# One weighting of the values for all heads in the even steps of a two-layer recurrent attention loop

## The chip, the cores and the metric

The kernel runs on one core of one Trainium2 chip. A core has TensorE (PE in the profile, its weight loads PEld), VectorE (DVE), ScalarE (ACT), GpSimd (POOL) and SyncE (SP), which here issues nearly all DMAs. TensorE writes its results to PSUM, which has eight banks of 512 fp32 numbers on each of 128 partitions; VectorE and ScalarE copy them to SBUF. The metric is the device time of one execution in microseconds (us).

## The reference, cut to what matters

Two layers, each of a recurrent attention with memory (A) and a dense block with relu (B), with the same weights in both, over 2048 tokens of 512 numbers.

```python
def _A_ref(x, mem0, Wq, Wk, Wv, Wo, seg_len):        # 32 heads of 128, M = 8 rows of memory, seg_len = 32
    mem = mem0
    for s in range(n_seg):                           # 64 segments
        xs = x[:, s * seg_len:(s + 1) * seg_len, :]
        h = jnp.concatenate([mem, xs], axis=1)       # L = 40 rows
        q, k, v = (jnp.einsum('btd,dhe->bhte', h, W) for W in (Wq, Wk, Wv))
        scores = jnp.where(mask, jnp.einsum('bhqe,bhke->bhqk', q, k) * scale, -1e9)
        o = jnp.einsum('bhqk,bhke->bhqe', softmax(scores), v)
        o = jnp.einsum('bhte,hed->btd', o, Wo)
        mem = o[:, :M, :]                            # handed to the next segment
        outs.append(o[:, M:, :])
    return jnp.concatenate(outs, axis=1)

x = x + _A_ref(_layernorm(x), ...)
x = x + _B_ref(_layernorm(x), B_w1, B_w2)            # relu(x w1) w2, inner width 1376
x = x + _A_ref(_layernorm(x), ...)
x = x + _B_ref(_layernorm(x), B_w1, B_w2)
```

A segment needs the memory that the one before it left, so the 64 segments of a layer follow each other.

## The kernel before, in words

The loop has 68 steps (`step(k)`, L801). In step k layer 0 works on segment k and layer 1 on segment k - 4 (`DELTA`), side by side: a = 0 and a = 1 are two columns blocks of 40 in the products of Q and K, two halves (rows 0 to 39 and 64 to 103) of the transposed probabilities and of the values `Vs`. The 32 heads are taken in two halves of 16, hf = 0 and hf = 1. In one step TensorE does, in this order:

- Q and K of the 16 heads of half 0 (`qp`, L663), in three batches, each copied out by ScalarE (Q) and VectorE (K);
- the values of the memory rows for all heads (`vp` from `rT`, L332), and in even steps those of layer 1's own segment (`values1`); they go by DMA through DRAM into the rows of `Vs`;
- the scores of half 0 (`sp`, L703); their exponents and probabilities follow on VectorE, ScalarE and GpSimd (L718 to L738);
- Q and K of half 1;
- the transposition of half 0's probabilities (`transpose_p`, L747), copied into `PT` in two parts, one by VectorE, one by ScalarE (L748);
- the scores of half 1;
- the weighting of the values of half 0 (`weighted_v`, `pv`, L762): for each head and layer one product of 40 rows and 40 columns, 32 matmuls in four banks;
- work of other kinds that fills the time until half 1's probabilities are there: the next values of layer 1 (`v1`), and where `fills_v0(k)` holds those of layer 0 three segments ahead (`v0`), products of the dense block (`dense_h`, `hp`; `dense_y`, `yp`), output projections (`output_x`, `wox`);
- the transposition of half 1, again into `PT`, a piece of filling work behind it, and the weighting of half 1;
- the projection of the memory rows of all heads (`output_mem`, `sp` from `OTm`, L710, written into the bank of layer 0's scores), whose result, copied by ScalarE and transposed (`mt`, L1097), becomes the memory of the next step (`HT`, L1100), with filling work in between.

The order on TensorE, VectorE, ScalarE and SP is that of the program text. Where the filling work lies is written out by hand: `places(i)` (L426) tells which heads of an output projection stand in which of four gaps of a step, and `hs` (L1010) does so for the 11 chunks of the dense block. The gaps are: after the values; between the second transposition and the weighting; after the memory projection; after `mt`.

Even steps are of two kinds. With k % 4 == 2 the step computes v0 and a whole dense_h and has no output projection; with k % 4 == 0 it has the rest of an output projection and neither v0 nor dense_h.

The weighted values of a head are split in the copies out of PSUM: the first `ahead(k, a)` columns (8, and 24 for layer 1 where k % 4 is 0 or 1 in most of the loop) go to `OTm` (`outputs_m`, L785), the others to `OTx0` (half 0) or `OTx1` (half 1) (`outputs_x`, L793). Half 0 is copied by ScalarE in both parts, half 1 by ScalarE for `OTm` and VectorE for `OTx1`.

PSUM: three banks `ps_c` (Q and K, transpositions, most weightings), two `ps_fill`, one `ps_wo` for the output projection, two for the scores (`sp_banks`). `VmS` of v0's second group is copied out by a function that is called later, behind the second transposition (L1027).

Of the kernel before, what the change touches and what calls it, by code (L numbers as in the profile page):

```python
# [22 lines left out]
def kernel(  # L23
# [327 lines left out]
    def values0(s, ii):  # L351

        if ii == 0:
            vds[0, s] = dram_values("vd0", "vd0", 4)
        t = tokens_T(s, 0, SEG)
        return group_values(lambda c4: t[:, c4, :], ii, vds[0, s], *((ps_fill, "fill") if ii else (ps_c, "c")), nc.sync,
                            "xn" if ii == 1 and s > 5 else "VmS", later=ii == 1 and s > 5)

    def values1(k, ii, place="VmS"):

# [58 lines left out]
    def fills_v0(k):  # L419

        return k % 2 == 0 and k + 3 < NSEG and k + 3 not in set_of

    def places(i):  # L426

        if i % 2 == 0:
            return (0, 10, 16, 24, H), (H,) * 5
        if i == NT - 1:  # L430
            return (0, 12, 12, 12, 12), (12, H, H, H, H)
        if fills_v0(2 * i + 2):
            return (0, 6, 10, 14, 20), (20, 23, 26, 30, H)
        return (0, 6, 10, 13, 16), (16, 23, 26, 30, H)

    def output_order(i):
# [301 lines left out]
        eng.tensor_tensor(out=P[:, :, 64 * a:64 * a + L], in0=es[:],  # L738
                          in1=sm[:].unsqueeze(2).to_broadcast([128, 8, L]), op=ALU.mult)

    def transpose_p():

        for p, copy in ((0, nc.vector.tensor_copy), (1, nc.scalar.copy)):
            tp = ps_c.tile([128, 4, 2, L], F32, tag="c")
            for sl in range(4):
                c = PL * (4 * p + sl)
                nc.tensor.matmul(tp[:, sl], lhsT=Pf[:, c:c + 128], rhs=ident_q, start=True, stop=True)  # L747
            copy(out=PT[:, 4 * p:4 * p + 4], in_=tp[:])  # L748

    def weighted_v(hf, act):  # L750
        pvs = {}
        for q in range(2):
            h0 = 16 * hf + 8 * q
            for a in act:
                pool, tag = (ps_fill, "fill") if (hf, q, a) in ((0, 0, 0), (1, 1, 1)) else (ps_c, "c")
                pvs[q, a] = pool.tile([128, 8, L], F32, tag=tag, name="pv")
            for hh in range(8):
                sl, g2 = divmod(8 * q + hh, 2)
                h = h0 + hh
                for a in act:  # L760
                    R = 64 * a
                    nc.tensor.matmul(pvs[q, a][:, hh, :], lhsT=Vs[R:R + L, h * Dh:(h + 1) * Dh],  # L762
                                     rhs=PT[R:R + L, sl, g2, :], start=True, stop=True)
        return pvs

# [35 lines left out]
    def step(k):  # L801
# [176 lines left out]
        with tc.high_priority(offset=PRIO):  # L978
            transpose_p()
            scores(qks[:2], act)  # L980
            scores(qks[2:], act)
            pvs = weighted_v(0, act)

            outputs_x(k, 0, pvs, 0, nc.scalar.copy)
            outputs_m(k, 0, pvs, 0)
            ess = exponents(act)


# [10 lines left out]
        if not apart:  # L999
            v1(1)  # L1000
        with tc.high_priority(offset=PRIO):
            outputs_m(k, 0, pvs, 1)
            outputs_x(k, 0, pvs, 1, nc.scalar.copy)
        v0(0)
        evict_v0 = v0(1)
        if k == 2:
            set_values(4, 3, 5)
            set_products(4, 5)
            set_store(4, nc.sync, 2, 4)
        hs = (0, 0, 4, 8, NFC) if fills_v0(k) else (0, 6, 8, 8, NFC) if len(act) == 1 else (0, 8, NFC, NFC, NFC)  # L1010
        if sooner is not None:
            dense_h(sooner, *hs[0:2])
        final = k == NSTEP - 1
# [6 lines left out]
        with tc.high_priority(offset=PRIO):  # L1020
            for a in act:
                probabilities(1, ess, a, k)
            if first:
                hand_on(dw)
            transpose_p()
            if evict_v0 is not None:
                evict_v0()  # L1027
            if k == 0:
                set_evict(3, 4)
                set_products(3, 5)  # L1030
            if k == 1:
# [12 lines left out]
        if nw is not None:  # L1044
            output_x(nw, *nx[1:3])
        with tc.high_priority(offset=PRIO):
            pvs = weighted_v(1, act)
            for q2 in range(2):
                if cont:
                    outputs_m(k, 1, pvs, q2)  # L1050
            head = act[:1] if nx is not None and nw % 2 == 0 else act
            outputs_x(k, 1, pvs, 0, nc.scalar.copy if final else nc.vector.tensor_copy, head)
            if first:
                block_normalize(dw)
            outputs_x(k, 1, pvs, 1, nc.vector.tensor_copy, head)
            for q2 in range(2):
                outputs_x(k, 1, pvs, q2, nc.vector.tensor_copy, [a for a in act if a not in head])
# [145 lines left out]
```

## Time and profile before

| | |
|---|---|
| runs (3) | 1613.30, 1613.77, 1613.97 us, median 1613.77 |
| profiled execution | 1612.95 us, of which the span from the first to the last instruction is 1611.2 |
| mean granted clock of TensorE | 1.000 |
| busy: TensorE, VectorE, ScalarE, GpSimd | 1597.3, 1082.3, 859.1, 267.6 us |
| steps 30, 31, 32, 33 | 23.86, 21.90, 23.24, 25.05 us |
| weighting, L762 | 4096 matmuls, 83.2 us busy |
| transposition, L747 | 1088 matmuls, 63.3 us busy |

A matmul of this kernel is recorded with its whole latency (176 to 380 ns), and the next one starts long before it ends; so busy TensorE time says little, and stretches are best measured from the first start of one group to the first start of the next. In the timeline a line stands for a run of like instructions: start and length in us, engine, line, operation, output and inputs with shapes, the count, and in brackets idle time of the engine before it and who ended it.

### The profile page before, as it was taken

How to read it: one execution, taken by the hardware profiler on the slowest of the kernel's cores; microseconds unless marked ns; L12 is line 12 of the kernel's file. 1: busy time of each engine (PE TensorE's matmuls, PEld its weight loads, DVE VectorE, ACT ScalarE, POOL GpSimd, SP SyncE). 2: the span in 40 equal slices, each digit the busy share in tenths (PEclk: the TensorE clock that was granted, in tenths of full speed). 3: DMA queues.
4: the chain of work that ended last, by engine and by line, in shares of the span. 5: the costliest groups of instructions: out<-in, count | busy, mean ns of one | idle time of the engine just before them, and what ended most of it. 6: DMA issues, size and time to landing. Idle time of an engine off the chain costs nothing.

```text
span 1611.2 us, 83133 instructions
## 1 busy us (share of the span) xinstructions
PE 1597.3 (99%) x37172; PEld 1175.3 (73%) x37172; DVE 1082.3 (67%) x2603; ACT 859.1 (53%) x2422; POOL 267.6 (17%) x510
## 2 busy tenths in 40 slices
PE   9999999999999999999999999999999999999998
PEld 4677777677777767777777777777777777777766
DVE  5556766776776677677667767666766767676655
ACT  4455555555555555555555555555555555555544
POOL 1112111111211111121111112111111211111100
PEclk9999999999999999999999999999999999999999
DMA  9732222222222222222322222222222222221111
GB/s 343 265 116 65 69 75 67 68 60 66 63 70 80 67 67 63 62 63 70 80 67 67 63 61 63 72 78 69 69 58 63 61 75 73 67 61 52 51 44 37
DMA packets 138309, 126.09 MB, mean 78 GB/s; under 512 B 43928, under 2 KB 126976, under 8 KB 137088
## 3 DMA queue, kind: packets, MB, share of 16 engines
q1 hardware_dynamic: 135296, 116.55, 24.8%
q8 instruction: 291, 4.77, 1.3%
q0 software_dynamic: 2560, 4.20, 1.0%
q14 instruction: 66, 0.54, 0.1%
q10 hardware_dynamic: 96, 0.04, 0.0%
HBM read 65.94 MB, written 45.35 MB: 69 GB/s over the span
## 4 chain that ended last, share of the span: by engine, by line
PE 95%; DVE 2%; DMA 1%; issue 1%; ACT 1%; POOL 0%; SPq 0%; DVEq 0%; ACTq 0%; POOLq 0%
PE qp L663 37%; PE vp L332 16%; PE sp L710 8%; PE wox L460 7%; PE hp L589 5%; PE yp L610 5%; PE pv L762 4%; PE wox L463 4%; PE sp L703 4%; PE tp L747 3%; PE vp L303 2%; DMA Wv_sb<-in_A_Wv_dram 0%; PE mt L1097 0%; PE tpx L648 0%; DVE PT L748 0%
## 5 line engine op out<-in xcount | busy, mean ns | idle before, releaser
L663 PE MATMUL qp<-HT,Wq_sb 128*128 128x80 bf16 (+1 forms) x8704 | 368.6, 199 | 0.9 <-DVE HT L1100 0.9
L663 PE MATMUL qp<-HT,Wk_sb 128*128 128x80 bf16 (+1 forms) x8704 | 367.7, 199 | 0.0
L663 PEld LDWEIGHTS <-Wq_sb 128*128 128x128 bf16 x8704 | 328.4, 99 | 19.9 <-issue 11.0
L663 PEld LDWEIGHTS <-Wk_sb 128*128 128x128 bf16 x8704 | 329.7, 99 | 0.8
L669 DVE CAST KT<-qp 128x480 bf16<-128x480 f32 (+3 forms) x340 | 199.4, 586 | 169.5 <-PE qp L663 163.5
L667 ACT CAST QT<-qp 128x480 bf16<-128x480 f32 (+3 forms) x340 | 172.4, 507 | 206.9 <-PE qp L663 206.1
L738 POOL TENSOR_TENSOR Pf<-es,sm 128x320 bf16<-128x320 f32 x187 | 135.3, 723 | 621.2 <-ACT QT L667 353.0
L337 ACT CAST VmS<-vp 128x512 bf16<-128x512 f32 x290 | 167.4, 588 | 117.6 <-PE vp L332 117.5
L718 DVE TENSOR_REDUCE mx<-sp 128x8 f32<-128x320 f32 x256 | 114.5, 486 | 115.6 <-PE sp L703 115.2
L729 ACT ACTIVATE es<-es 128x320 f32<-128x320 f32 x256 | 111.0, 469 | 75.3 <-DVE es L721 69.2
L735 DVE TENSOR_REDUCE sm<-es 128x8 f32<-128x320 f32 x256 | 120.5, 471 | 23.5 <-ACT es L729 13.0
L710 PE MATMUL sp<-Wo_sb,OTm 128*32 128x512 bf16 x2144 | 128.2, 380 | 0.0
L332 PE MATMUL vp<-Wv_sb,rT 128*32 128x512 bf16 x2144 | 128.0, 380 | 0.1
L460 PE MATMUL wox<-Wo_sb,OTx 128*128 128x512 bf16 x480 | 122.8, 380 | 0.0
L332 PE MATMUL vp<-Wv_sb,HT 128*32 128x512 bf16 x2048 | 122.5, 380 | 0.0
L721 DVE TENSOR_TENSOR es<-sp,mx 128x320 f32<-128x320 f32 x256 | 113.1, 480 | 0.5
L231 POOL TENSOR_TENSOR rstd<-rstd,mhalf_t 128x1 f32<-128x1 f32 x85 | 47.0, 553 | 397.9 <-DVE rstd L230 397.9
L793 DVE CAST OTx<-pv 128x256 bf16<-128x256 f32 x255 | 85.3, 385 | 36.5 <-ACT OTm L785 35.7
L785 ACT CAST OTm<-pv 128x64 bf16<-128x64 f32 x510 | 92.9, 252 | 30.9 <-PE pv L762 30.9
L748 ACT CAST PT<-tp 128x320 bf16<-128x320 f32 x136 | 58.3, 429 | 72.3 <-PE tp L747 70.1
L793 ACT CAST OTx<-pv 128x256 bf16<-128x256 f32 (+1 forms) x257 | 79.0, 362 | 28.6 <-PE pv L762 28.6
L748 DVE CAST PT<-tp 128x320 bf16<-128x320 f32 x136 | 66.8, 491 | 38.3 <-PE tp L747 37.2
(138 smaller groups left out, 1934.0 us busy)
## 6 DMA issues: line engine op xcount, KB each, us to landing
vd<-VmS SPq DMA_DIRECT2D x156, 128.0 KB
Vs<-vd SPq DMA_DIRECT2D x156, 128.0 KB
vmd<-VmS SPq DMA_DIRECT2D x134, 128.0 KB
Vs<-vmd SPq DMA_DIRECT2D x254, 32.0 KB
Vs<-vmd SPq DMA_DIRECT2D x120, 64.0 KB
Vs<-vset SPq DMA_DIRECT2D x19, 256.0 KB
Wv_sb<-in_A_Wv_dram SPq DMA_DIRECT2D x4, 1024.0 KB
Wq_sb<-in_A_Wq_dram SPq DMA_DIRECT2D x4, 1024.0 KB
```

What stands on the lines that cost most here:

```text
L332: nc.tensor.matmul(vp[32 * j:32 * j + 32, :], lhsT=lhsT(c4), rhs=Wv_sb[:, c4, n * 512:(n + 1) * 512], start=(c4 == 0), stop=(c4 == NC4 - 1 ...
L337: nc.scalar.copy(out=VmS[:], in_=vp[:])
L460: nc.tensor.matmul(wo_tiles[i][:], lhsT=ot, rhs=Wo_sb[:, h, :], start=(n == 0), stop=(n == H - 1))
L663: nc.tensor.matmul(qp[:, hi, 0:ncol], lhsT=W_sb[:, c4, h * Dh:(h + 1) * Dh], rhs=HT[:, c4, a_lo:a_hi, :], start=(c4 == 0), stop=(c4 == NC4 ...
L667: nc.scalar.copy(out=dst[:, 0:nh, a_lo * L:a_hi * L], in_=qp[:, 0:nh, 0:ncol])
L669: nc.vector.tensor_copy(out=dst[:, 0:nh, a_lo * L:a_hi * L], in_=qp[:, 0:nh, 0:ncol])
L710: nc.tensor.matmul(wo[32 * j:32 * j + 32, :], lhsT=OTm[:, h, :], rhs=Wo_sb[:, h, :], start=(h < 4), stop=(h >= H - 4), tile_position=(0, 3 ...
L718: nc.vector.tensor_reduce(out=mxs[a][:], in_=sp_tiles[a], axis=AX.X, op=ALU.max)
L735: nc.vector.tensor_reduce(out=sm[:], in_=es[:], axis=AX.X, op=ALU.add)
L738: eng.tensor_tensor(out=P[:, :, 64 * a:64 * a + L], in0=es[:], in1=sm[:].unsqueeze(2).to_broadcast([128, 8, L]), op=ALU.mult)
L748: copy(out=PT[:, 4 * p:4 * p + 4], in_=tp[:])
L793: copy(out=ot[:, 8 * q:8 * q + 8, c:c + n], in_=pvs[q, a][:, :, L - n:L])
```

## The change

In the even steps from 4 to 60 (`joint(k)`) the weighting of half 0 no longer follows the second scores. Both halves are weighted in one stretch behind the second transposition (`joint_v`): 64 matmuls in the order of the heads, twelve heads to a bank, so three banks for each layer. Five of the six are taken from `ps_c`, `ps_fill` and, with k % 4 == 2, `ps_wo`; the sixth is the bank of layer 1's scores. Half 1's transposed probabilities get a tile of their own, a buffer of the tag `es`, as half 0's are still needed.

All copies out of these banks follow the stretch in the program: first the `OTm` part of bank (0, 1) on VectorE, the five others on ScalarE, and then the parts for `OTx0` and `OTx1`, one of them on ScalarE and seven on VectorE. In these steps the filling work between the second transposition and the weighting moves ahead of the transposition (four chunks of `dense_h`, or three heads of `output_x`), and the later copy of v0's second group is done at once. Odd steps, and the first and last even ones, keep their order.

```diff
-                            "xn" if ii == 1 and s > 5 else "VmS", later=ii == 1 and s > 5)
+                            "xn" if ii == 1 and s > 5 else "VmS", later=ii == 1 and s > 5 and not joint(s - 3))
+    def joint(k):
+        return k % 2 == 0 and DELTA <= k < NSEG - 2
     def places(i):
-        if fills_v0(2 * i + 2):
-            return (0, 6, 10, 14, 20), (20, 23, 26, 30, H)
+        if joint(2 * i + 2):
+            return (0, 6, 10, 13, 16), (16, 26, 26, 30, H)
         return (0, 6, 10, 13, 16), (16, 23, 26, 30, H)
...
-    def transpose_p():
+    PTs = {}
+    def transpose_p(hf=0, apart=False):
+        PTs[hf] = wk.tile([128, 8, 2, L], BF, tag="es", bufs=2, name="PT1") if apart else PT
...
-            copy(out=PT[:, 4 * p:4 * p + 4], in_=tp[:])
+            copy(out=PTs[hf][:, 4 * p:4 * p + 4], in_=tp[:])
...
+    def joint_v(k):
+        pvs = {}
+        for j in range(3):
+            for a in range(2):
+                if (j, a) == (1, 1):
+                    t = sp_banks[1]
+                else:
+                    where = (ps_c, "c") if (j, a) in ((0, 0), (2, 0), (2, 1)) else (ps_fill, "fill")
+                    if k % 4 == 2 and (j, a) == (0, 1):
+                        where = (ps_wo, "wo")
+                    t = where[0].tile([128, 512], F32, tag=where[1], name="pv")
+                pvs[j, a] = t[:, 0:12 * L].rearrange("p (h l) -> p h l", h=12)
+        for h in range(H):
+            hf, (sl, g2) = h // 16, divmod(h % 16, 2)
+            for a in range(2):
+                R = 64 * a
+                shared = (h // 12, a) == (1, 1)
+                nc.tensor.matmul(pvs[h // 12, a][:, h % 12, :], lhsT=Vs[R:R + L, h * Dh:(h + 1) * Dh],
+                                 rhs=PTs[hf][R:R + L, sl, g2, :], start=not shared or h == 12, stop=True,
+                                 skip_group_check=shared)
+        return pvs
+    def joint_m(k, pvs, j, a, copy):
+        h0, h1, n = 12 * j, min(12 * j + 12, H), ahead(k, a)
+        copy(out=OTm[:, h0:h1, a * M:a * M + n], in_=pvs[j, a][:, 0:h1 - h0, 0:n])
+    def joint_x(k, pvs, j, a, copy):
+        h0, h1, n = 12 * j, min(12 * j + 12, H), L - ahead(k, a)
+        c = 64 * a + SEG * (k % 2)
+        for ot, lo, hi in ((OTx0[:, k // 2 % 2], 0, 16), (OTx1, 16, H)):
+            u, v = max(h0, lo), min(h1, hi)
+            if u < v:
+                copy(out=ot[:, u - lo:v - lo, c:c + n], in_=pvs[j, a][:, u - h0:v - h0, L - n:L])
...
             scores(qks[2:], act)
-            pvs = weighted_v(0, act)
-            outputs_x(k, 0, pvs, 0, nc.scalar.copy)
-            outputs_m(k, 0, pvs, 0)
+            if not joint(k):
+                pvs = weighted_v(0, act)
+                outputs_x(k, 0, pvs, 0, nc.scalar.copy)
+                outputs_m(k, 0, pvs, 0)
             ess = exponents(act)
...
-            outputs_m(k, 0, pvs, 1)
-            outputs_x(k, 0, pvs, 1, nc.scalar.copy)
+            if not joint(k):
+                outputs_m(k, 0, pvs, 1)
+                outputs_x(k, 0, pvs, 1, nc.scalar.copy)
...
-        hs = (0, 0, 4, 8, NFC) if fills_v0(k) else (0, 6, 8, 8, NFC) if len(act) == 1 else (0, 8, NFC, NFC, NFC)
+        hs = (0, 4, 4, 8, NFC) if joint(k) else (0, 0, 4, 8, NFC) if fills_v0(k) else ...
...
-            transpose_p()
+            transpose_p(1, joint(k))
...
-            pvs = weighted_v(1, act)
...
+            if joint(k):
+                pvs = joint_v(k)
+                joint_m(k, pvs, 0, 1, nc.vector.tensor_copy)
+                for j, a in ((0, 0), (1, 0), (1, 1), (2, 0), (2, 1)):
+                    joint_m(k, pvs, j, a, nc.scalar.copy)
+                for j in range(3):
+                    for a in range(2):
+                        joint_x(k, pvs, j, a, nc.scalar.copy if (j, a) == (2, 0) else nc.vector.tensor_copy)
+            else:
+                pvs = weighted_v(1, act)
...
```

More of the change, by code (lines that the diff above doesn't have):

```diff
@@ L762, in weighted_v @@
                     nc.tensor.matmul(pvs[q, a][:, hh, :], lhsT=Vs[R:R + L, h * Dh:(h + 1) * Dh],
-                                     rhs=PT[R:R + L, sl, g2, :], start=True, stop=True)
+                                     rhs=PTs[hf][R:R + L, sl, g2, :], start=True, stop=True)
         return pvs
+    def joint_v(k):
[29 more added lines that the diff above has]
+                copy(out=ot[:, u - lo:v - lo, c:c + n], in_=pvs[j, a][:, u - h0:v - h0, L - n:L])
     def ride_of(k):
@@ L1009, in step @@
             set_store(4, nc.sync, 2, 4)
-        hs = (0, 0, 4, 8, NFC) if fills_v0(k) else (0, 6, 8, 8, NFC) if len(act) == 1 else (0, 8, NFC, NFC, NFC)
+        hs = (0, 4, 4, 8, NFC) if joint(k) else (0, 0, 4, 8, NFC) if fills_v0(k) else (0, 6, 8, 8, NFC) if len(act) == 1 else (0, 8, NFC, NFC, NFC)
         if sooner is not None:
@@ L1046, in step @@
         with tc.high_priority(offset=PRIO):
-            pvs = weighted_v(1, act)
[L1048 to L1057, printed above, removed]
+            if joint(k):
[8 more added lines that the diff above has]
+                pvs = weighted_v(1, act)
+                for q2 in range(2):
+                    if cont:
+                        outputs_m(k, 1, pvs, q2)
+                head = act[:1] if nx is not None and nw % 2 == 0 else act
+                outputs_x(k, 1, pvs, 0, nc.scalar.copy if final else nc.vector.tensor_copy, head)
+                if first:
+                    block_normalize(dw)
+                outputs_x(k, 1, pvs, 1, nc.vector.tensor_copy, head)
+                for q2 in range(2):
+                    outputs_x(k, 1, pvs, q2, nc.vector.tensor_copy, [a for a in act if a not in head])
             if back is not None and place(back)[1]:
```

## The prediction

> **What bounds the kernel now.** I read the totals and the chain of the page first, then the waits of TensorE, then the timeline of two even steps. The page says how full TensorE is, and how much of the chain that ended last lies on it:
>
> ```profile
> PE 1597.3 (99%) x37172; PEld 1175.3 (73%) x37172; DVE 1082.3 (67%) x2603; ACT 859.1 (53%) x2422; POOL 267.6 (17%) x510
> ...
> PE 95%; DVE 2%; DMA 1%; issue 1%; ACT 1%; POOL 0%; SPq 0%; DVEq 0%; ACTq 0%; POOLq 0%
> ```
>
> TensorE works for 1597.3 of 1611.2 us. A change can win only by giving TensorE less to do, or lose only by making it wait. The waits of TensorE name no large one; this is the largest that comes back:
>
> ```profile
> PE tp L747 <- DVE Pf L738: 1.3, 3, 0.7
> ```
>
> So every number below is a distance between starts on TensorE. The timeline of step k = 30 (723.89 to 747.75 us), from the first transposition on; columns are start, length, engine, line, operation, tiles, count:
>
> ```profile
> 737.38 0.48 PE L747 MATMUL tp<-ident,Pf 128*128 128x80 bf16 x8
> ...
> 737.79 0.57 PE L703 MATMUL sp<-KT,QT 128*40 128x40 bf16 x32
> ...
> 738.30 0.64 PE L762 MATMUL pv<-PT,Vs 40*128 40x40 bf16 x32
> ...
> 738.86 1.91 PE L332 MATMUL vp<-Wv_sb,HT 128*32 128x512 bf16 x32
> ...
> 742.43 0.46 PE L747 MATMUL tp<-ident,Pf 128*128 128x80 bf16 x8
> 742.73 1.06 PE L589 MATMUL hp<-dnT,w_sb 128*128 128x128 bf16 x16
> 742.78 0.49 DVE L748 CAST PT<-tp 128x320 bf16<-128x320 f32 x1 [0.57 <-PE tp L747]
> 742.98 0.43 ACT L748 CAST PT<-tp 128x320 bf16<-128x320 f32 x1
> ...
> 743.72 0.59 PE L762 MATMUL pv<-PT,Vs 40*128 40x40 bf16 x32
> 743.82 0.60 ACT L595 ACTIVATE hT<-hp 128x512 bf16<-128x512 f32 x1
> 744.23 1.91 PE L710 MATMUL sp<-Wo_sb,OTm 128*32 128x512 bf16 x32
> ...
> 746.08 1.07 PE L589 MATMUL hp<-dnT,w_sb 128*128 128x128 bf16 x16
> ...
> 746.98 0.25 PE L1097 MATMUL mt<-sel,wm_sb 128*128 128x32 bf16 x4
> ```
>
> Two things are to be seen. The same 16 products of the dense layer take 0.99 us ahead of the weighting (742.73 to 743.72) and 0.90 ahead of mt (746.08 to 746.98): a change of the array's tile shape costs about 0.09. Eight transpositions take 0.41 ahead of the scores and 0.30 ahead of hp: the same, 0.11. And a weighting of 16 heads takes 0.51 to 0.56, of which 0.10 is such a change at its end and about 0.05 a slower start in the longer ones; 0.40 is left, 0.025 per head. In step k = 32 the dense layer is replaced by the output projection wox:
>
> ```profile
> 783.97 0.63 PE L762 MATMUL pv<-PT,Vs 40*128 40x40 bf16 x32
> ...
> 784.53 1.91 PE L332 MATMUL vp<-Wv_sb,HT 128*32 128x512 bf16 x32
> ...
> 786.38 1.69 PE L460 MATMUL wox<-Wo_sb,OTx 128*128 128x512 bf16 x7
> ...
> 787.27 0.62 DVE L738 TENSOR_TENSOR Pf<-es,sm 128x320 bf16<-128x320 f32 x1
> ...
> 787.99 0.45 PE L747 MATMUL tp<-ident,Pf 128*128 128x80 bf16 x8
> 788.27 0.81 PE L460 MATMUL wox<-Wo_sb,OTx 128*128 128x512 bf16 x3
> ...
> 789.02 0.65 PE L762 MATMUL pv<-PT,Vs 40*128 40x40 bf16 x32
> 789.60 1.91 PE L710 MATMUL sp<-Wo_sb,OTm 128*32 128x512 bf16 x32
> ```
>
> Seven wox take 1.61 us though four take 0.87 later in the step (0.217 each, 1.52 for seven): 0.09 is a wait for the probabilities, whose last product ends at 787.89, 3.92 after the scores.
>
> **The change part by part.** It touches the even steps 4 to 60, 29 of them: 15 with k divisible by 4 (as 32), 14 others (as 30). No matmul is added or removed. I compare the stretch from the end of the second scores to the start of the memory projection (sp from OTm).
>
> Steps like 30, before: 744.23 - 738.30 = 5.93. After: the values of the two groups as now (738.86 to 742.43, 3.57), then the 16 products of the dense layer moved ahead of the transposition, followed by a stretch of their own tile shape (0.90), then the transposition followed by the weighting (0.41), the slower start (0.05), 32 heads (0.81) and the change at the end (0.10): 5.84, so 0.09 less if nothing waits. But two waits lose their cover. VectorE's half of the second transposition's copy starts 0.35 after the transposition and lasts 0.49: ready at 0.84, with 0.04 to be seen by TensorE 0.88. The heads that need it come up at 0.41 + 0.05 + 0.40 = 0.86. That costs 0.02. ScalarE's half now stands behind the relu of the 16 dense products, which end as the transposition begins: relu from 0.20 for 0.60 (743.82 row), its successor about 0.10 before its end as these records overlap, so 0.70 to 1.13, seen at 1.17. The last eight heads come up at 0.88 + 0.20 = 1.08 and wait 0.09. So 1.17 + 0.20 + 0.10 = 1.47 after the transposition, 3.57 + 0.90 + 1.47 = 5.94 in all: nothing gained (0.01 lost). Bounds: from 0.14 gained (no wait, no slow start) to 0.40 lost (relu and copy each a full length later by a queue on ScalarE).
>
> Steps like 32, before: 789.60 - 783.97 = 5.63. After: values 1.85, ten wox 2.17, so the transposition could begin at 4.02, and the probabilities, whose chain on VectorE starts with the scores and is not touched, allow it at 4.02 (787.99 - 783.97). Then 0.41 + 0.05 + 0.81 + 0.10: 5.39, or 0.24 less. No relu stands in ScalarE's way here (its half ends at 0.97). What is late next is the memory projection: its first head needs the memory columns of all twelve heads of bank (0, 1), 288 values a partition that VectorE copies first. Their last product comes at 0.41 + 0.05 + 0.30, its result 0.18 later (the 176 ns of a matmul in L762), the copy starts at 0.98 and lasts some 0.43 (256 elements 0.385 on the page, 320 elements 0.49): seen at 1.46, against 1.37 for the end of the weighting. So 4.02 + 1.46 = 5.48, 0.15 gained. Bounds: 0.24 (copy in time) and 0.10 lost (copy and projection 0.34 later, the whole of the copies ahead of it in one queue).
>
> The evictions. ScalarE has eight copies mid-step and four at the end (4 of OTx, 8 of OTm), and then none mid-step and six at the end; VectorE goes from four of 256 elements (1.42 us in a row) to one of OTm and seven of OTx, about 2.6 us, over at 3.6 after the transposition in steps like 30 and 3.3 in those like 32, there with 0.69 for the riders' sum at every other: 4.0. The next work on VectorE that TensorE needs is the copy of mt into HT, ready 1.84 + 0.90 + 0.2 behind the projection's start, at 4.4: hidden with 0.4 to spare; without that cover a step would lose what the copies run over. Of the six banks the last are free when VectorE is through, a whole microsecond before the next step's second Q and K product needs them. The second half of the scores' bank is read before the next masks, on VectorE in order. I cost all this at nothing.
>
> Queues. The eviction of the second new value group moves from behind the transposition's copy to ahead of the relu on ScalarE: its 0.59 starts 0.9 before the transposition and ends 0.3 before, so nothing is pushed; if it were late it would push relu and copy. Its DMA is issued on SP's queue one microsecond earlier; nothing else on SP moves, as the loads of the next values wait for the second weighting before and after. Only the loads of their lower half, which could start behind the first weighting, now start up to 2 us later, still some 12 us ahead of their use. POOL is not passed by anything. The dense products start 0.86 earlier: their input, a transposing DMA issued at 735.99 with the products at 742.73, is then used 5.9 us after its issue, and in odd steps such products run 5.6 us after it without a wait. The rest: nothing.
>
> Sum: 15 x 0.15 - 14 x 0.01 = 2.1 us less. The profiled execution took 1612.95 us (span 1611.2), the median of the runs shown is 1613.77; 0.8 of difference is not the change's. 1613.77 - 2.1 = 1611.7.
>
> A rule that speaks against the change: the Trainium skill, TensorEngine Tiling (Array Packing), Performance Considerations, PSUM Bottleneck, says that packing the array speeds up the products but not the emptying of PSUM, which may then become the bound. It states no price; what it would do here is the third rival.
>
> **The rivals.** Measurements of this kernel can tell about 0.2% from no change, 3.2 us; 1610.5 and 1617.0 are the marks.
>
> First, the waits stay hidden: the memory columns and both halves of the copy come in time. For it: weightings with one satisfied wait show no gap, and the first weighting already starts 0.51 behind its transposition without a long one. Against: the cover shrinks to 0.45 by the same rows. Gain 15 x 0.24 + 14 x 0.09 = 4.9: 1608.9.
>
> Second, ScalarE's half is later than I think in steps like 30: eviction, relu and copy behind each other without overlap, 0.40 more than my 1.13. For it: three operations now stand in a row that before had the copy first. Against: the eviction has 0.3 to spare. 14 x 0.40 = 5.6: 1617.3, just slower. It decides from 0.38 per step on.
>
> Third, the emptying of PSUM sets the end. The memory projection takes twelve heads in 1.84 x 12/32 = 0.69; ScalarE copies two banks for them, so from 0.345 per copy on the projection runs at ScalarE's pace. At 0.40 it loses 0.11 for each of three pairs, 0.33 x 29 = 9.6: 1621.3, slower. For it: all copies now come behind the products instead of half. Against: four OTm copies of 64 elements take 0.56 together in step 30 and four of mixed size 0.78 in step 32. (This is the skill's rule; by the trace so far the copies keep up.)
>
> **How the numbers follow.** The forecast 0.46, the first rival 0.30, the second 0.11, the third 0.13. Forecast 1611.7; for it alone 1610.5 to 1615.5. The range 1608.4 to 1617.5 reaches from the first rival (with half a microsecond for the start that may cost nothing) to the second, and leaves out the third and a little of the ends. Faster by over 0.2%: 0.30; within: 0.46; slower: 0.24.
>
> **What would show it.** Right: one weighting of 64 products per even step of about 0.9 to 1.1 us; steps like 32 shorter by 0.1 to 0.2, steps like 30 unchanged; a gap at the heads 16 or 24 in steps like 30; the first OTm copy on VectorE ending about when the weighting does. Wrong: a gap at the start of the memory projection in steps like 30, at the copy of HT, in the odd steps, or at the transposition; steps like 30 changed by more than 0.15 either way.

## The result, and the profile after

The changed kernel takes 1618.88 us (median of 7 runs, 1618.32 to 1620.88) against 1613.97 for the kernel before beside it (7 runs, 1613.06 to 1614.49). The ratio is 1.0034 with the interval 1.0023 to 1.0046: slower by a third of a per cent, 4.9 us, where 2.1 us less was forecast. The profiled execution has a span of 1616.6 us, 5.4 more than before. The totals of the page after, and its chain that ended last by engine:

```profile
PE 1587.9 (98%) x37086; PEld 1176.8 (73%) x37172; DVE 1116.9 (69%) x2719; ACT 829.9 (51%) x2248; POOL 267.0 (17%) x510
...
PE 89%; DVE 4%; issue 2%; DMA 2%; ACT 2%; SPq 0%; POOL 0%; ACTq 0%; DVEq 0%; POOLq 0%
```

The work is the same (37172 loads of weights, as before), and TensorE's share of the chain falls from 95% to 89%: time is lost in waits. The waits of TensorE in the changed kernel look as if they said where, and they do not:

```profile
PE yp L616 <- issue: 4.9, 31, 0.2
PE wox L466 <- issue: 4.8, 30, 0.2
```

The page counts 37086 matmuls for 37172 loads: 86 records are missing, mostly first records of a stretch, and the hole where one should be is then shown as a wait for "issue" (a wait for which the profile shows no releaser). The stretches of yp and wox last as long as before. What can be trusted is again distances between starts. The steps 30, 31, 32 and 33 as windows, with the length of the step in the second column and TensorE's busy time behind the comma:

```profile
725.49:749.69 24.20, 24.12 (x611) 18.72 (x609) 17.29 (x42) 13.20 (x32) 4.08 (x9) 1.00 0.41 109
749.69:771.65 21.96, 21.64 (x500) 16.17 (x501) 16.30 (x39) 11.45 (x38) 3.31 (x6) 1.00 0.08 22
771.65:794.87 23.22, 22.90 (x547) 16.61 (x548) 16.01 (x41) 11.50 (x30) 3.98 (x8) 1.00 0.43 106
794.87:819.99 25.12, 24.96 (x559) 18.61 (x559) 17.98 (x43) 13.10 (x39) 5.22 (x10) 1.00 0.11 31
```

Before, the same four steps took 23.86, 21.90, 23.24 and 25.05. Over all steps from 8 to 60, medians in us by class of step (the classes named by one member; the number of changed steps, or of odd steps behind them, in brackets):

| steps like | before | after | change x steps |
|---|---|---|---|
| 30 (14) | 23.862 | 24.196 | +4.7 |
| 31 (14) | 21.903 | 21.966 | +0.9 |
| 32 (15) | 23.220 | 23.216 | -0.1 |
| 33 (15) | 25.052 | 25.091 | +0.6 |

Added step by step instead of by medians it is +4.3, +0.9, -0.2 and +0.8, and -0.5 at the start and the end: 5.4, the difference of the spans. The loss has three places: most in steps like 30, some in the odd steps, which the change does not touch, and a gain in steps like 32 that did not come. The timeline of the changed kernel in step 30, from the second value group to the copy of HT:

```profile
741.35 0.87 ACT L735 ACTIVATE es<-es 128x320 f32<-128x320 f32 x2 [1.41 <-DVE es L727]
...
741.64 2.15 PE L332 MATMUL vp<-Wv_sb,xnT 128*32 128x512 bf16 x32
...
742.13 1.54 ACT L337 CAST VmS<-vp 128x512 bf16<-128x512 f32 x3
...
743.72 1.07 PE L595 MATMUL hp<-dnT,w_sb 128*128 128x128 bf16 x16
...
744.63 0.45 PE L757 MATMUL tp<-ident,Pf 128*128 128x80 bf16 x8
744.83 0.60 ACT L601 ACTIVATE hT<-hp 128x512 bf16<-128x512 f32 x1 [0.41 <-PE hp L595]
...
745.01 0.49 PE L797 MATMUL pv<-PT,Vs 40*128 40x40 bf16 x25
745.04 0.49 DVE L758 CAST PT<-tp 128x320 bf16<-128x320 f32 x1 [1.22 <-PE tp L757]
745.32 0.42 ACT L758 CAST PT<-tp 128x320 bf16<-128x320 f32 x1
...
745.58 0.18 PE L797 MATMUL pv<-PT,Vs 40*128 40x40 bf16 x1
...
745.68 0.18 PE L797 MATMUL sp<-PT,Vs 40*128 40x40 bf16 x1
...
746.17 1.91 PE L716 MATMUL sp<-Wo_sb,OTm 128*32 128x512 bf16 x32
...
749.21 0.23 DVE L1158 CAST HT<-mt 128x64 bf16<-128x64 f32 x1 [0.88 <-PE mt L1155]
```

Two holes are to be seen. The 32 products on xnT last 2.15; the same form on HT lasts 1.91. In the middle of them TensorE waits 0.25, until ScalarE has emptied a bank: the first copy of the x3 row, which starts at 742.13 and takes 0.57. It stands in ScalarE's program order behind the two exponentials of 741.35, for which ScalarE had waited 1.41. And in the weighting the first product of head 16 starts at 745.58 and its partner at 745.68, though 32 products from 745.01 on, at 0.0125 each, would bring it up at 745.41. The copy of HT has an idle VectorE ahead of it (0.88): the evictions at the end are not late.

### The profile page after: what moved, and what is told of

The parts are those of the page before. It is cut to its first block, busy times and chain, and to the rows that moved or that the text cites. A ratio compares the mean times of both kernels' runs of the same rounds, so it can differ in the third digit from the quotient of the medians.

```text
span 1616.6 us, 83061 instructions
## 1 busy us (share of the span) xinstructions
PE 1587.9 (98%) x37086; PEld 1176.8 (73%) x37172; DVE 1116.9 (69%) x2719; ACT 829.9 (51%) x2248; POOL 267.0 (17%) x510
## 4 chain that ended last, share of the span: by engine, by line
PE 89%; DVE 4%; issue 2%; DMA 2%; ACT 2%; SPq 0%; POOL 0%; ACTq 0%; DVEq 0%; POOLq 0%
PE qp L669 37%; PE vp L332 14%; PE wox L466 6%; PE sp L716 6%; PE hp L595 5%; PE yp L616 4%; PE wox L469 4%; PE sp L709 4%; PE tp L757 3%; PE pv L772 2%; PE pv L797 2%; PE vp L303 1%; DVE OTx L841 1%; DMA dnT<-xn 1%; ACT VmS L337 1%
## 5 line engine op out<-in xcount | busy, mean ns | idle before, releaser
L466 PE MATMUL wox<-Wo_sb,OTx 128*128 128x512 bf16 x434 | 110.0, 379 | 7.3 <-issue 4.8
L595 PEld LDWEIGHTS <-w_sb 128*128 128x128 bf16 (+1 forms) x1452 | 79.6, 100 | 13.3 <-issue 13.1
L332 PEld LDWEIGHTS <-HT 128*32 128x32 bf16 x2048 | 53.1, 97 | 48.7 <-ACT rT L1167 0.4
L595 PE MATMUL hp<-dnT,w_sb 128*128 128x128 bf16 (+2 forms) x1452 | 88.2, 217 | 0.2 <-ACT VmS L337 0.2
```

What stands on the lines that cost most here:

```text
L332: nc.tensor.matmul(vp[32 * j:32 * j + 32, :], lhsT=lhsT(c4), rhs=Wv_sb[:, c4, n * 512:(n + 1) * 512], start=(c4 == 0), stop=(c4 == NC4 - 1 ...
L466: nc.tensor.matmul(wo_tiles[i][:], lhsT=ot, rhs=Wo_sb[:, h, :], start=(n == 0), stop=(n == H - 1))
L595: nc.tensor.matmul(hp[0:fs, fi, r0:r1], lhsT=w1_sb[:, c4, fc * 128:fc * 128 + fs], rhs=xnT[:, c4, r0:r1], start=(c4 == 0), stop=(c4 == NC4 ...
```

## The experiments

All are the changed kernel with the edits shown or named; none leaves work out, and e4, e6 and e7 add two products to a joint stretch. A cover is work on TensorE during which another engine gets ready, so that no wait is seen. Each batch has its own runs of the kernel before: medians 1613.83 for e1 to e4, 1612.94 for e5 to e8, 1613.61 for e9 to e11.

**e1: one half of the change alone.** Only steps like 32 are joined.

```diff
-        return k % 2 == 0 and DELTA <= k < NSEG - 2
+        return k % 4 == 0 and DELTA <= k < NSEG - 2
```

> The joint weighting only where k is divisible by 4; steps 6, 10 to 58 as before. My theory (two waits in the steps k % 4 == 2: 0.25 us at the values of v0, 0.25 us at head 16; in those with k % 4 == 0 only the second, paid by what the joining saves): the joint steps cost nothing (median step 23.22 us as before), so 1614.0 within 1 us, ratio 0.9995 to 1.0005. Rival (the bunched copies out of PSUM slow every joint step and the odd steps behind it): half of the loss stays, 1616.5.

Measured: 1614.71, ratio 1.0007 (0.9998 to 1.0016). Steps like 30 are back at 23.862 and the odd steps behind them at 21.903; steps like 32 (23.216) and the odd ones behind them (25.090) are as in the changed kernel. So joining in steps like 32 brings nothing and costs 0.04 in the next step, and the rest of the loss belongs to the steps like 30 and the odd ones behind them.

**e2: another bank for the second value group.** It takes a bank of the pool "c" in place of the "fill" bank that the first group of v1 has just left.

```diff
-        return group_values(..., *((ps_fill, "fill") if ii else (ps_c, "c")), nc.sync,
+        return group_values(..., *((ps_fill, "fill") if ii and not joint(s - 3) else (ps_c, "c")), nc.sync,
```

> The second value group of v0 goes to a ps_c bank instead of ps_fill in joint steps; all else as changed. My theory: its bank was the one that the first v1 group left, whose copy on ScalarE stands behind the exponents, so the wait of 0.25 us in 14 steps goes: 3.6 us less than the changed kernel, 1615.3; steps k % 4 == 2 take 23.94 instead of 24.20 us. Rival (ScalarE itself is late, whatever bank): the wait moves to the next bank and the time stays at 1618.9.

Measured: 1615.30, 1.0009 (1.0000 to 1.0018). Step 30 in the timeline of e2:

```profile
740.50 0.87 ACT L735 ACTIVATE es<-es 128x320 f32<-128x320 f32 x2 [1.41 <-DVE es L727]
...
740.78 1.90 PE L332 MATMUL vp<-Wv_sb,xnT 128*32 128x512 bf16 x32
...
741.27 2.05 ACT L337 CAST VmS<-vp 128x512 bf16<-128x512 f32 x4
```

The exponentials stand ahead of the eviction as they did, but nothing waits for it: 1.90 in place of 2.15, and the class falls from 24.196 to 23.945. This one wait is 0.25 x 14 = 3.5 us, the largest part of the loss. Before the change the same eviction (copy out of a bank) stood behind the same exponentials, as step 30 of the kernel before shows:

```profile
739.75 0.87 ACT L729 ACTIVATE es<-es 128x320 f32<-128x320 f32 x2
...
740.52 1.06 ACT L337 CAST VmS<-vp 128x512 bf16<-128x512 f32 x2
740.60 1.90 PE L332 MATMUL vp<-Wv_sb,xnT 128*32 128x512 bf16 x32
```

Its time hangs on the second scores (737.79 in the kernel before): the copy starts 2.73 behind their first product in both kernels. But TensorE came to the bank 0.565 later before the change, because the first weighting lay between, and found it free with some 0.3 to spare. The change took the weighting away and with it the cover.

**e3: another place for the second PT.** PT1 leaves the ring of two buffers in which the exponentials work ("es") and takes one buffer each of the K and Q rings.

```diff
-        PTs[hf] = wk.tile([128, 8, 2, L], BF, tag="es", bufs=2, name="PT1") if apart else PT
+        if apart:
+            PTs[hf] = [wk.tile([128, HB, 2 * L], BF, tag=nm, bufs=3, name=nm)[:].rearrange("p a b -> p (a b)")[:, 0:8 * L]
+                       .rearrange("p (s g l) -> p s g l", s=4, g=2) for nm in ("KT", "QT")]
+        else:
+            PTs[hf] = [PT[:, 0:4], PT[:, 4:8]]
...
```

The lines left out index the two parts where they are written and read.

> The second half's transposed probabilities go in two parts to buffers of the K and Q copies instead of a buffer of the exponents. My theory: the added 0.06 and 0.04 us of the odd steps, and 0.06 of the 0.41 us that VectorE's copy starts behind the transposition, come from waits that the exponents' two buffers now need: odd steps back to 21.90 and 25.05 us (1.4 us in all) and up to 0.06 in each of 29 even steps (1.7): 1616.0. Rival (odd steps are late because the copies of the joint banks run into them): odd steps stay at 21.97 and 25.09, 1617 to 1619.

Measured: 1616.91, 1.0017 (1.0008 to 1.0026). The odd steps are back at their old length; steps 31 and 33 as windows of e3:

```profile
749.25:771.15 21.90, 21.90 (x502) 16.09 (x501) 16.30 (x39) 11.41 (x38) 3.32 (x6) 1.00 0.07 22
...
794.35:819.40 25.05, 25.05 (x560) 18.58 (x559) 17.94 (x43) 13.01 (x39) 5.23 (x10) 1.00 0.11 30
```

What the ring did can be counted. The view of the exponentials' line has, in the changed kernel,

```profile
L735 ACT ACTIVATE es<-es x256: 469/470/473, 34.2 to 1601.7; 128x320 f32<-128x320 f32 x128
L735 ACTq EVENT_SEMAPHORE  x95: 17/17/17, 80.6 to 1597.5; - x95
```

and in e3:

```profile
L735 ACTq EVENT_SEMAPHORE  x81: 17/17/17, 81.4 to 1595.9; - x81
```

The kernel before has 81 too. One more use of the ring in a step moves the exponentials to the other buffer. In the 14 steps like 31 the second exponential of a pair then gets a semaphore instruction of its own; behind it ScalarE's copy of Q is 0.06 late, and the next batch of products (of K) with it. In steps like 33 the number of these instructions stays at one, but it stands in front of the second exponential instead of the first, and the copy of Q is 0.07 late in step 33; the class loses 0.04. On VectorE the copy into PT1 also had a separate wait in each of the 29 steps: besides TensorE's products it has to wait for POOL, the last user of its buffer.

```profile
L758 DVEq EVENT_SEMAPHORE  x29: 21/21/21, 130.2 to 1452.2; - x29
```

That row is of the changed kernel; e3 has none. VectorE's copy starts 0.34 after the transposition in e3, 0.41 in the changed kernel. Steps like 30 gain 0.067 by it, steps like 32 only 0.018: their projection is then held by the OTm copy of 288 values (0.46, over 1.38 after the transposition in e3), the wait that the forecast had put there.

**e4: the waits of the stretch taken at its start.** Two products of head 24 are added ahead of the stretch, into the banks that heads 24 on will use, so that the waits for those heads are over before head 16.

```diff
+        for a in range(2):
+            R = 64 * a
+            nc.tensor.matmul(pvs[2, a][:, 0, :], lhsT=Vs[R:R + L, 24 * Dh:25 * Dh], rhs=PTs[0][R:R + L, 0, 0, :],
+                             start=True, stop=True)
```

> Two products of head 24 with the first half's probabilities are added at the start of the joint stretch, and overwritten later; they take the waits for the loads of the upper half of the values there. My theory: of the 0.25 us lost at head 16 some 0.10 is these waits one by one in the middle of the stretch, though the loads landed long before: 0.10 less and 0.03 more work in each of 29 steps, 2 us less than the changed kernel, 1616.9. Rival (all 0.25 is the copy of the transposition, the waits are hidden by it): 0.03 more in 29 steps, 1619.6.

Measured: 1641.25, 1.0171 (1.0157 to 1.0185), far from both. Its timeline in step 30:

```profile
755.90 0.49 DVE L758 CAST PT<-tp 128x320 bf16<-128x320 f32 x1 [1.22 <-PE tp L757]
756.18 0.42 ACT L758 CAST PT<-tp 128x320 bf16<-128x320 f32 x1
756.44 0.18 PE L793 MATMUL pv<-PT,Vs 40*128 40x40 bf16 x1 [0.39 <-DVE PT L758]
...
756.65 0.58 PE L801 MATMUL pv<-PT,Vs 40*128 40x40 bf16 x25
```

The banks of heads 24 on are those of the second transposition, so my two products had to wait for the copies out of them: one starts 0.05 after VectorE's copy ends (756.39), the stretch 0.05 after ScalarE's (756.60). It says nothing on the waits in the middle. But it prices something else: with both halves of that copy uncovered a step is 0.76 longer (like 32) or 0.65 (like 30).

**e5: e2 and e3 together, and two of the dense products' four chunks kept behind the transposition** in steps like 30.

```diff
-        hs = (0, 4, 4, 8, NFC) if joint(k) else ...
+        hs = (0, 2, 4, 8, NFC) if joint(k) else ...
```

> The new bank for v0's second group and the buffers of K and Q for the transposed probabilities together, and in steps k % 4 == 2 two of the four dense chunks go back between the second transposition and the weighting. My theory (two covers were lost: the time till the probabilities are ready and the time of the transposition's copy): half of the chunks fill each, so steps k % 4 == 2 take 4.06 + 0.30 + 0.55 + 1.00 = 5.91 us from the second scores to the memory projection against 5.94 before, 23.83 in all; those with k % 4 == 0 23.20; odd ones as before: 1613.8 - 14 x 0.03 - 15 x 0.02 = 1613.1. Rival (the copies out of the joint banks set the end): steps k % 4 == 2 stay over 23.87, 1614.5 or more.

Measured: 1611.55, 0.9993 (0.9984 to 1.0002): steps like 30 came out 0.07 better than expected, steps like 32 (23.199) as expected. Step 30 of e5:

```profile
740.44 0.62 PE L595 MATMUL hp<-dnT,w_sb 128*128 128x128 bf16 x8
...
741.11 0.45 PE L761 MATMUL tp<-ident,Pf 128*128 128x80 bf16 x8
...
741.39 0.61 PE L595 MATMUL hp<-dnT,w_sb 128*128 128x128 bf16 x8
741.45 0.49 DVE L762 CAST KT<-tp 128x320 bf16<-128x320 f32 x1 [0.49 <-PE tp L761]
...
741.94 0.49 PE L801 MATMUL pv<-PT,Vs 40*128 40x40 bf16 x25
...
742.88 0.83 PE L716 MATMUL sp<-Wo_sb,OTm 128*32 128x512 bf16 x12
```

Eight dense products now hide VectorE's copy, and the whole stretch takes 0.94 (741.94 to 742.88), with no hole at head 16 or 24. Steps like 30 take 23.762, 0.10 less than before the change: about what the forecast has as the saving of a joint stretch without waits (0.09). In steps like 32, where it has 0.24, no version comes near it: the best one below takes 23.148 against 23.220 before.

**e10: e2 and e3 without the third edit.**

> The new bank and the buffers of K and Q, without moving dense chunks back. My theory (the causes add up): steps k % 4 == 2 at 24.20 - 0.25 - 0.07 = 23.88, k % 4 == 0 at 23.20, odd ones as before: 1613 by the kernel before at 1613, ratio 1.000. It leaves the wait for the transposition's copy, 0.11 of it in steps k % 4 == 2 that the run with both does not have. Rival (the gain of the run with both comes from these two alone): 23.77, 0.1% under the kernel before.

Measured: 1612.35, 0.9993 (0.9984 to 1.0001); steps like 30 at 23.876, like 32 at 23.200. The two causes add up: 24.196 - 23.876 = 0.320, and 0.251 + 0.067 singly. It leaves steps like 30 within 0.02 of before. The remaining 0.11 against e5 lies behind the transposition: the joint stretch takes 1.09 here and 0.94 in e5, less 0.04 for the dense products split in two. Only the steps show this (14 x 0.11 = 1.6 us): the ratios of e5 and e10 to the kernel before beside them are the same, 0.9993, and their intervals are wider than the difference.

**e6: the waits of the late heads taken at the start of the stretch.** e5, and the two added products of e4 into the banks of head 0, which nothing holds; they read values that were loaded for the late heads. So only waits that are long satisfied move to the start.

```diff
+        for a in range(2):
+            R = 64 * a
+            nc.tensor.matmul(pvs[0, a][:, 0, :], lhsT=Vs[R:R + L, 24 * Dh:25 * Dh], rhs=PTs[0][0][R:R + L, 0, 0, :],
+                             start=True, stop=True)
```

> As the run with both, and two products of head 24 with the first half's probabilities at the start of the joint stretch, this time into the bank of the first heads, which is free there, overwritten by head 0. My theory: the second wait at head 16, 0.10 us from the first to the second of its products, is for loads that landed long before, and goes: steps k % 4 == 2 0.08 less than without; in steps k % 4 == 0 the projection then waits for VectorE's copy of the memory columns, 0.02 less at most: 1.2 us less than the run with both, 1611.9. Rival (the 0.10 is TensorE's start after a wait for the copy, whichever semaphore): 0.025 more per step, 1613.8.

Measured: 1615.84, 1.0015 (1.0006 to 1.0024), 4.3 more than e5 where it should have been less. Step 32:

```profile
790.45 0.45 PE L761 MATMUL tp<-ident,Pf 128*128 128x80 bf16 x8
...
790.86 0.30 PE L797 MATMUL pv<-PT,Vs 40*128 40x40 bf16 x2
...
791.11 0.60 PE L805 MATMUL pv<-PT,Vs 40*128 40x40 bf16 x25
```

The waits did not vanish, they moved to the start, and step 32 shows it at its worst: the first four products start at 0.41, 0.54, 0.66 and 0.79 after the transposition, 0.125 apart instead of the usual 0.0125, and the step takes 0.39 more than in e5. In nine of the fourteen steps like 32 from 8 to 60 the first three products start at 0.38, 0.38 and 0.42 and only the fourth is late, by 0.10. Step 36 is one of them:

```profile
885.27 0.45 PE L761 MATMUL tp<-ident,Pf 128*128 128x80 bf16 x8
...
886.31 0.46 DVE L812 CAST OTm<-pv 128x288 bf16<-128x288 f32 x1 [0.20 <-PE pv L805]
...
886.91 0.83 PE L716 MATMUL sp<-Wo_sb,OTm 128*32 128x512 bf16 x12 [0.16 <-ACT OTm L812]
```

Here the theory was half right. The hole at head 16 is gone, and the last product of the stretch starts 0.07 sooner than in e5 (1.30 after the transposition instead of 1.37). But the 0.10 at the start also delays bank (0, 1), so VectorE's copy of it starts 1.04 after the transposition instead of 0.92, and the projection behind it 1.64 instead of 1.52. (The row puts that wait down to ScalarE's copies; e7 shows that it is VectorE's.) The median step like 32 is 0.13 longer. Steps like 30 are 0.025 longer, which is what two products take: the wait instructions are through there before the stretch begins, while the eight dense products run. The medians add up to 2.3 of the 4.3 us. The rest is not explained; in the profiled execution, which is 5.7 longer than that of e5, step 4 alone is 1.7 longer.

The trace shows how such a wait costs. Each of the weight loads in question has two events to wait for, and one of them is a semaphore instruction of its own in the queue of the weight loads. In e6 the starts of these instructions are 0.125 apart, or a little more: in step 36 at 0.03, 0.16, 0.28 and 0.41 after the transposition, where the fourth comes too late for a stretch that can start at 0.38; in step 30 at 0.08, 0.23, 0.36 and 0.48, all before the stretch starts at 0.83. At head 16 of the changed kernel the instruction starts only as the first product is released (745.58), the load follows 0.07 later and the product at 745.68; in e5 it starts at 742.12, 0.21 ahead of its load, and nothing waits. The loads of the values themselves were issued over 6 us before. So my reading that such waits are free if taken early holds only where there is time for them. Why the later ones start so late in step 32 is not settled.

**e7: e6 with the two OTm copies of the first banks exchanged** in steps like 32: ScalarE takes the one of 288 values, VectorE the one of 96.

```diff
-                joint_m(k, pvs, 0, 1, nc.vector.tensor_copy)
-                for j, a in ((0, 0), (1, 0), (1, 1), (2, 0), (2, 1)):
+                joint_m(k, pvs, 0, 1 if k % 4 == 2 else 0, nc.vector.tensor_copy)
+                for j, a in ((0, 0 if k % 4 == 2 else 1), (1, 0), (1, 1), (2, 0), (2, 1)):
```

> As the run before it, and in steps k % 4 == 0 ScalarE copies the 288 memory columns of bank (0, 1) and VectorE the 96 of bank (0, 0). My theory: in these steps the memory projection waits for VectorE's copy (0.46 us, over 1.38 after the transposition); ScalarE begins sooner and takes 0.40, so the projection starts 0.08 sooner in 15 steps: 1.2 us less than the run before it, 1610.7, and below the kernel before the change. Rival (the projection waits for TensorE's own drain): no difference.

Measured: 1612.54, 0.9997 (0.9988 to 1.0005): steps like 32 fall by 0.17 against e6 (23.331 to 23.162), so with the added products VectorE's OTm copy had been the last to end. The exchange brought more than the 1.2 expected of it (15 x 0.17 = 2.5); the total still misses the expected 1610.7 by 1.8, because that was reckoned from 1611.9 for e6 and not from its 1615.84.

**e9: the exchange on e5, without the added products.**

> The run with both, and the exchange of the first two copies in steps k % 4 == 0, without the two added products. My theory: these steps wait 0.04 to 0.05 us at the memory projection for VectorE's copy; they go from 23.20 to 23.16, steps k % 4 == 2 stay at 23.76: 0.7 us less than the run with both, 0.13% under the kernel before. Rival (the exchange gains only where the added products delayed the stretch): 23.20, no difference to the run with both.

Measured: 1610.96, 0.9982 (0.9973 to 0.9991). It is faster than the changed kernel and than the one before, the latter by 0.18%. Steps like 32 fall from 23.199 in e5 to 23.148, as expected. Step 32 of e9:

```profile
786.49 0.45 PE L761 MATMUL tp<-ident,Pf 128*128 128x80 bf16 x8
...
787.37 0.26 DVE L808 CAST OTm<-pv 128x96 bf16<-128x96 f32 x1
787.41 0.69 ACT L808 CAST OTm<-pv 128x288 bf16<-128x288 f32 x2
...
787.96 0.40 PE L716 MATMUL sp<-Wo_sb,OTm 128*32 128x512 bf16 x4
```

The projection starts 1.47 after the transposition, against 1.54 in the changed kernel and 1.52 in e3.

**e11: e9 with three of four chunks ahead of the transposition** (`hs = (0, 3, 4, 8, NFC)`), to hide the copy with less.

> As the run with the exchange alone, with three chunks ahead of the second transposition and one behind. My theory: with two, TensorE still waits 0.05 us for the probabilities (4.07 after the scores against 4.02 of work); with three it doesn't, and one chunk (0.22) with the change of shape (0.10) and the first half's heads (0.40) still covers the copy (0.89): 0.04 less in 14 steps, 0.6 us less than the run with the exchange alone. Rival (the copy of the second part on ScalarE comes behind the relu then): 0.1 more per step, 1.4 us more.

Measured: 1611.46, 0.9988 (0.9979 to 0.9996), 0.5 more than e9 instead of 0.6 less. Steps like 30 are at 23.829, 0.064 above e9. The timeline of e11 in step 30:

```profile
741.77 0.60 ACT L601 ACTIVATE hT<-hp 128x512 bf16<-128x512 f32 x1
...
742.26 0.39 ACT L808 CAST OTm<-pv 128x96 bf16<-128x96 f32 x2
...
742.55 0.12 PEld L716 LDWEIGHTS <-OTm 128*32 128x32 bf16 x8 [0.17 <-ACT OTm L808]
```

With one chunk less behind the transposition the last product of the stretch starts 0.22 sooner after it than in e9. But ScalarE's relu, and the first OTm copy behind it, come only 0.07 sooner, and the projection waits for that copy: one wait exchanged for another. It is not the rival's wait: ScalarE's half of the transposition's copy still ends (0.97) about where the relu starts (0.86), as in e9.

**e8: the filling work back in its old place.** The dense products and wox between transposition and weighting as before the change, and the eviction of the second value group behind the transposition's copy.

```diff
-                            "xn" if ii == 1 and s > 5 else "VmS", later=ii == 1 and s > 5 and not joint(s - 3))
+                            "xn" if ii == 1 and s > 5 else "VmS", later=ii == 1 and s > 5)
...
-            return (0, 6, 10, 13, 16), (16, 26, 26, 30, H)
+            return (0, 6, 10, 13, 16), (16, 23, 26, 30, H)
...
-        hs = (0, 4, 4, 8, NFC) if joint(k) else ...
+        hs = (0, 0, 4, 8, NFC) if joint(k) else ...
```

> The changed kernel with the filling work of both kinds of even step back where it was, behind the second transposition, and the later copy of v0's second group. My theory: the first weighting was the cover of the softmax chain, which ends 4.06 us after the second scores; without it and with the filling work behind the transposition, TensorE waits there 0.65 us in steps k % 4 == 0 and 0.2 in the others, the wait at head 16 goes down to 0.1: steps of 23.70 (k % 4 == 0) and 24.28, so 15 x 0.48 + 14 x 0.42 + 1.4 more than before, 1628. Rival (the copy of the transposition is all that is lost): steps of 23.05 and 24.0, 1615.

Measured: 1628.33, 1.0096 (1.0080 to 1.0111). That the total is the expected 1628 is partly luck: steps like 32 take 23.841 (expected 23.70) and steps like 30 24.205 (24.28). Step 32 of e8:

```profile
794.09 0.62 DVE L744 TENSOR_TENSOR Pf<-es,sm 128x320 bf16<-128x320 f32 x1
...
794.85 0.45 PE L757 MATMUL tp<-ident,Pf 128*128 128x80 bf16 x8 [0.54 <-POOL rT L1150]
795.13 0.81 PE L466 MATMUL wox<-Wo_sb,OTx 128*128 128x512 bf16 x3
...
795.88 0.49 PE L797 MATMUL pv<-PT,Vs 40*128 40x40 bf16 x25
```

The weighting no longer waits for the copies (0.75 of wox lie between), but TensorE waits ahead of the transposition until the probabilities are there (VectorE's last product ends at 794.71), 4.06 after the second scores, as in steps like 32 of the changed kernel. (The row names POOL's copy of rT; in steps like 30 of e8, which have no such copy there, the transposition starts at the same 4.06.) So moving that work forward was not a loss by itself: it covers the probabilities, which the first weighting had covered till then. The work can stand in only one of the two places, and the first weighting had filled both.

## Why the prediction was wrong

Point by point, by the prediction's own steps.

- *"The evictions … I cost all this at nothing"*: this is the step that failed. The prediction followed the six banks of the weighting and the copies at the end, all of which are indeed in time (HT's copy finds VectorE idle), and asked of the second value group's eviction only whether it would push something (*"its 0.59 starts 0.9 before the transposition … so nothing is pushed"*). The eviction of the group before it, which frees the bank for the second, stands behind exponentials tied to the scores, and TensorE reached the bank 0.565 earlier. That costs 0.25 per step like 30, 3.5 us, and without it the changed kernel takes 1615.30 (e2). The term of the sum is *"the values of the two groups as now"*, 3.57; they took 3.83.
- *Head 16, "That costs 0.02"*: the mechanism was right, the size was off. The stretch starts 0.08 earlier than forecast (0.38 after the transposition, not 0.41 and a slow start of 0.05), and 32 products take 0.40 as forecast, so head 16 comes up at 0.78 instead of 0.86; VectorE's half is 0.06 later, through PT1's ring (e3); and the partner's separate wait comes behind it. The hole is 0.17 before the first product and 0.10 before its partner, less one ordinary pitch: some 0.25 in all 29 steps. So the first rival, in which all waits stay hidden, was wrong too.
- *The last eight heads, 0.09*: did not occur; ScalarE's half, with relu ahead of it, ends at 1.11 and the heads come up later than that, because of the hole at head 16. The second rival had put a further 0.40 there: none of it.
- *Steps like 32, 5.63 to 5.48*: measured 5.61 to 5.605. The transposition starts at 4.06, not 4.02: the probabilities end 3.92 after the scores in both kernels, but the transposition follows 0.146 behind them where it was 0.10; why is not settled. The projection starts 1.54 behind it in place of 1.46. What ends last is the weighting, held up at head 16, and not the OTm copy, which is the term the forecast had used. With the hole narrowed (e3) the OTm copy does take over, at 1.52.
- *Steps like 30, 5.93 to 5.94*: measured 5.94 to 6.27, that is 0.26 in the values and 0.07 behind the transposition.
- *The odd steps*: the prediction named them among what would show it wrong and costed them at nothing. It did not look at whose ring the new PT1 takes a buffer of: 0.06 and 0.04 per odd step, 1.5 us (e3 gives back both).
- *Third rival, PSUM*: no. The Trainium skill, TensorEngine Tiling (Array Packing), Performance Considerations, PSUM Bottleneck, says that the emptying of the banks may become the bound behind packed products. In the changed kernel the trace does not show this: the weighting itself ends last. A copy out of a bank sets the start of the projection only in the versions that have the waits cut down, and exchanging two copies is then worth 0.05 per step like 32, from e5 (23.199) to e9 (23.148).

By the terms: steps like 30 came out 0.33 above the forecast (6.27 for 5.94), 14 x 0.33 = 4.6; steps like 32 0.125 (5.605 for 5.48), 15 x 0.125 = 1.9; the odd steps 1.5. Together 8.0, less 0.5 at the start and the end: 7.5, which is the 2.1 of the forecast gain and the 5.4 of the spans. Of the 4.6, the bank is 3.5.

## What to carry to other kernels

Before a stretch of work is taken out of the critical engine's order, list every wait of that engine *behind* it and ask by how much each event was early: what the stretch covered becomes visible, even where the trace of before shows no wait at all. Follow each bank and each ring buffer by its last user, not only by its own new user; an extra allocation in a shared ring changes who waits for whom one step later. A reordering that lost may be worth keeping with its covers put back: here two allocations, eight moved products and one exchange of copies turned +0.34% into -0.18% (0.9982, 0.9973 to 0.9991).

## What the runs showed of the hardware

A wait whose event is long past is not free for TensorE among short products. Where a weight load had a second event to wait for, the wait was a separate instruction, and these started 0.125 apart or a little more (e6). They cost nothing while earlier work ran (e6, steps like 30: four of them behind the transposition's start, in front of eight dense products; e5: no hole in the stretch), 0.10 where one came too late (e6, most steps like 32; head 16 of the changed kernel), and in step 32 of e6 they spaced four products 0.125 apart instead of 0.0125.

One more use of a ring of two buffers showed up as 14 further semaphore instructions on ScalarE and as 0.06 on TensorE in the next step, with no row among TensorE's waits that names the ring. Where only the place of the instruction changed, in front of the second exponential instead of the first, it was 0.04.
